# Attention and two expert stages on one core: new numbers in a planner that sets each engine's order, with other costs for short products and for routing

## The chip, the core and the metric

The kernel runs on one NeuronCore of a Trainium2 chip. Five engines work side by side, each through its own queue in program order: PE (TensorE, matrix products and transposes into PSUM), DVE (VectorE), ACT (ScalarE), POOL (GpSimd, which also issues the indirect transfers), and SP (SyncE, which issues the other transfers). An engine whose next instruction waits for a semaphore does nothing else, whatever stands behind it. The metric is the device time of one execution in microseconds (us); less is better.

## The reference

Three parts in a row. The third sends each of the 3072 tokens to one of 8 experts with 384 places each, in the order of the gate's values.

```python
# attention: 4 x 8 heads, 768 positions, 64 wide
k_sum = k.reshape(B, H, nb, 32, D).max(axis=3)
v_sum = v.reshape(B, H, nb, 32, D).mean(axis=3)
scores_s = scale * np.einsum('bhsd,bhnd->bhsn', q, k_sum) + np.log(32)
scores_l = np.where(np.abs(pos[:, None] - pos[None, :]) < 16, scale * np.matmul(q, k.transpose(0, 1, 3, 2)), -1e9)
a = softmax(np.concatenate([scores_l, scores_s], axis=-1))
x = np.matmul(a, np.concatenate([v, v_sum], axis=2))     # then to 3072 x 512
...
x = (((x @ w1) * (x @ w2)) @ w3) @ w_out                 # 512 -> 1024 -> 1024 -> 512
...
# experts: logits = x @ w_gate; largest values first, a token once, 384 tokens to an expert
for e in range(8):
    out[mask_e] = np.maximum(x[mask_e] @ w1[e], 0.0) @ w2[e]
```

## The kernel before, in words

The big products are exact to float32 by splitting each operand into a high and a low float32r part (`x_h`, `x_l` for the activations, `w12_h`, `w12_l` for w1 and w2, `split_e` for expert weights) and adding three products, h·h, h·l and l·h. A long product is 128x512 (or 128x384, 128x256); the short ones are attention's, the transposes and routing's.

**Stages.** Attention runs in 16 head pairs of 3 steps, 48 steps `n`. Per pair: `transposes` of K and Q on PE into banks 0 and 1, then `evac_kmax` and `evac_kedge` on DVE and `evac_k`, `evac_q` on ACT, which empty those banks. Per two steps `s_mm` (scores). Per step: `s_min` (DVE), four `s_exp1` (ACT), `s_inv` (DVE), `s_norm` (POOL), `p_tr` (transpose on PE into bank 4), `p_evac` (ACT, out of bank 4). Per two steps `pv_mm`, then two `xt` copies. Once all steps that touch a chunk of 512 tokens are done for a head pair kt (0 to 3), `x_h` (ACT) and `x_l` (DVE) make its two parts, and `ab_mm(c, ft, m, kt)` multiplies it by w1 (m=0) and w2 (m=1): six chunks c, eight column tiles ft, three long products a call. `ab_a` and `ab_b` empty their banks. In the same stretch the 64-bit w1 and w2 words are narrowed (`narrow_y` on ACT, `narrow` on DVE).

Then w3·w_out is multiplied out (`wmm`), the logits are made, and routing runs: seven searches by bisection, each of three or four rounds of `compare` (DVE), `count` (PE), `full` (DVE), `count_full` (PE), `narrower` (DVE), with `bound` behind the first round, and `which_full`, `spread_full` (PE), `choose` (DVE) at the end of a search. In the gaps PE takes `row_mm`, the products that give the experts' input rows: 480 of 512 columns (t up to 19) and then 192 of 256 columns. Each finished tile is put (`row_put`, ACT) and stored to DRAM (`row_store`, SP); `gather` (POOL) fetches the rows of an expert in two halves of three transfers, once `places_end` (DVE) has the indices. Behind routing come `turn` (transposes of gathered rows), `up_mm`, `down_mm`, `scatter` for eight experts.

**What sets the order.** All operations are put in a list with a time of their own, `t`, an engine, a duration and the names that they read and write. `schedule` plays this list through: each engine that is free takes the ready operation with the smallest `t`, and is then busy for the duration. The order in which they were taken is emitted, engine by engine; nothing is reordered on the chip. `t` comes from the step, from `CFG` and from `OFF`, one number per function. `CFG` also says which engine takes a copy (`xdve`, `pdve`, `kedge`, `xl`, `wl12`).

Of the kernel before, what the change touches and what calls it, by code (L numbers as in the profile page):

```python
# [46 lines left out]
SHARED = ("narrow", "vb_sum", "x_l", "s_sub", "s_half", "s_norm", "k_spread", "wconv_l", "w12_l", "abh_l", "split_e", "wph_put")  # L47


def schedule(ops, free):  # L50
# [39 lines left out]
    now, done, port = 0.0, [], 0.0  # L90
# [25 lines left out]
def fused_kernel(tc, q, k, v, moe_w1, moe_w2, moe_w3, moe_w_out, w_gate, ew1, ew2, out):  # L116
    nc = tc.nc
    with ExitStack() as ctx:
# [167 lines left out]
        def evac_q(j):  # L286
            nc.scalar.activation(QT[j % 2], turned_qk("q", j)[:, 0:768], AF.Copy, scale=-0.125)
# [262 lines left out]
        for j in range(-1, NJ):  # L550
# [8 lines left out]
            if J < NJ:  # L559
# [14 lines left out]
            for n in range(m, m + 3):  # L574
                P, SB, VB_ = ("P", n % NP), [s_bank(0), s_bank(1)], pv_bank(n)
                if n % 2 == 0:
                    kq = [(x, i % 2) for i in sorted({n // 3, (n + 1) // 3}) for x in ("Kw", "Ke", "Kg", "Ks", "Q")]
                    op(n, PE, 1.02, kq, SB, s_mm, n // 2)
# [3 lines left out]
                if not C["pacc"] or n % C["pacc"]:  # L582
# [11 lines left out]
                dve = C["pdve"] and n % C["pdve"] == 0  # L594
# [774 lines left out]
```

## Time and profile before

| what | value |
|---|---|
| time, median of 3 runs | 943.7 us (941.36 to 944.99) |
| the profiled execution | 939.69 us, its span 937.9 us |
| PE busy | 879.5 us, 94% of the span |
| DVE, ACT, POOL busy | 482.0, 408.7, 262.1 us |
| TensorE's granted clock, mean | 0.99 |

The span runs from the first to the last instruction. A granted clock of 1.00 is 2.4 GHz and 0.50 is 1.2 GHz; a value between is a mean over a stretch with both. PE is called busy while a product or transpose is in it, so a share of 94% says where PE waits, not that its work could not be quicker.

### The profile page before, as it was taken

Reading aid. Unit: us, or ns where it says so; the run is one execution under the profiler, and the core shown is the slowest. Engines: PE = TensorE matmul, PEld = TensorE weight load, DVE = VectorE, ACT = ScalarE, POOL = GpSimd, SP = SyncE. Lnnn points to the kernel's source line nnn. Section 1 sums busy time; section 2 is a strip of 40 time slices with the busy share of each in tenths; the row PEclk is TensorE's granted clock in tenths of the full one; section 3 lists DMA queues with packets and bytes.
Section 4 is the critical chain, followed back from the end, with each engine's and each line's share of the span. In section 5 each row is a group of like instructions: output and inputs, shape, how many; then the busy total and the mean of one; then the engine's idle time right before and its main releaser. Section 6 shows DMA issues by size and latency. Waiting matters only on the chain.

```text
span 937.9 us, 16023 instructions
## 1 busy us (share of the span) xinstructions
PE 879.5 (94%) x5899; PEld 731.2 (78%) x5899; DVE 482.0 (51%) x1351; ACT 408.7 (44%) x987; POOL 262.1 (28%) x280
## 2 busy tenths in 40 slices
PE   2687999999999999999999999999999999999994
PEld 2465887888888887777776667689898998899893
DVE  4887997846556641111316666663465355445110
ACT  1787888985443251111224142322465345445220
POOL 4535344432011000000027384535513313301001
PEclk9989999999999999999999999999999999999997
DMA  9999988733343200000003134113656446454001
GB/s 231 224 213 206 226 191 158 153 82 110 116 120 122 74 1 1 1 0 1 1 1 113 61 120 135 35 45 96 199 209 216 135 157 207 142 169 147 23 13 36
DMA packets 143335, 105.22 MB, mean 112 GB/s; under 512 B 103312, under 2 KB 117648, under 8 KB 143248
## 3 DMA queue, kind: packets, MB, share of 16 engines
q1 hardware_dynamic: 139024, 91.53, 36.4%
q0 software_dynamic: 4224, 12.59, 3.8%
q8 instruction: 48, 0.79, 0.4%
q14 instruction: 39, 0.32, 0.1%
HBM read 89.15 MB, written 12.58 MB: 108 GB/s over the span
## 4 chain that ended last, share of the span: by engine, by line
PE 84%; DVE 7%; DMA 3%; ACT 2%; SPq 1%; issue 1%; POOL 0%; POOLq 0%; ACTq 0%; DVEq 0%
PE PS L499 28%; PE PS L1233 14%; PE PS L1247 13%; PE PS L1127 11%; PE PS L448 5%; PE PS L373 2%; PE PS L358 2%; PE PS L318 2%; PE PS L265 2%; PE PS L633 1%; DMA w_dt.float<-in_k_dram 1%; PE PS L1217 1%; DVE w_dt.float L853 1%; PE PS L435 1%; PE PS L465 1%
## 5 line engine op out<-in xcount | busy, mean ns | idle before, releaser
L499 PE MATMUL PS<-w_dt.float32r,w_dt.float32r 128*128 128x512 f32 x1152 | 283.4, 397 | 0.6 <-ACT w_dt.float L269 0.4
L499 PEld LDWEIGHTS PS<-w_dt.float32r,w_dt.float32r 128*128 128x128 f32 x1152 | 210.7, 188 | 50.4 <-issue 7.1
L1127 PE MATMUL PS<-w_dt.float32r,w_dt.float32r 128*128 128x512 f32 (+1 forms) x672 | 143.9, 367 | 0.0
L1233 PE MATMUL PS<-w_dt.float32r,w_dt.float32r 128*128 128x384 f32 x768 | 135.5, 335 | 0.9 <-ACT w_dt.float32r L1222 0.5
L1233 PEld LDWEIGHTS PS<-w_dt.float32r,w_dt.float32r 128*128 128x128 f32 x768 | 133.4, 188 | 2.4 <-ACT w_dt.float32r L1222 1.0
L1247 PE MATMUL PS<-w_dt.float32r,w_dt.float32r 128*128 128x512 f32 x576 | 135.0, 392 | 0.0
L1104 POOL TENSOR_TENSOR w_dt.float32r<-w_dt.float,w_dt.float32r 128x512 fp32r<-128x512 f32 x48 | 61.4, 1301 | 240.9 <-issue 185.6
L1247 PEld LDWEIGHTS PS<-w_dt.float32r,w_dt.float32r 128*128 128x128 f32 x576 | 107.0, 188 | 21.7
L1127 PEld LDWEIGHTS PS<-w_dt.float32r,w_dt.float32r 128*128 128x128 f32 x672 | 109.6, 190 | 15.8 <-issue 0.8
L1184 DVE TENSOR_TENSOR w_dt.float32r<-w_dt.float,w_dt.float32r 128x512 fp32r<-128x512 f32 x112 | 72.3, 687 | 61.5 <-ACT w_dt.float32r L1182 60.5
L506 DVE TENSOR_TENSOR w_dt.float<-w_dt.float,PS 128x512 f32<-128x512 f32 x48 | 32.9, 686 | 121.3 <-PE PS L499 117.1
L1182 ACT ACTIVATE w_dt.float32r<-w_dt.float 128x512 fp32r<-128x512 f32 x128 | 73.6, 625 | 15.2 <-DMA w_dt.float<-in_moe_w_dram 11.3
L502 ACT ACTIVATE w_dt.float<-PS 128x512 f32<-128x512 f32 x48 | 28.6, 597 | 114.3 <-PE PS L499 114.2
L335 ACT ACTIVATE w_dt.float<-w_dt.float,w_dt.float 128x120 f32<-128x120 f32 x192 | 73.7, 388 | 4.3 <-DVE w_dt.float L324 4.3
L1241 DVE SCALAR_TENSOR_TENSOR w_dt.float32r<-PS,w_dt.float32r 128x384 fp32r<-128x384 f32 x64 | 35.5, 556 | 74.2 <-ACT w_dt.float32r L1239 74.2
L1202 POOL DMA_INDIRECT w_dt.float<-moe_rows,w_dt.float x48 | 47.1, 981 | 84.6 <-PE PS L1217 65.4
L354 POOL TENSOR_TENSOR w_dt.float<-w_dt.float,w_dt.float 128x480 f32<-128x480 f32 x48 | 50.6, 1058 | 61.1 <-DVE w_dt.float L351 47.4
L1254 POOL DMA_INDIRECT out_dram<-w_dt.float,w_dt.float x24 | 25.2, 1049 | 139.1 <-ACT w_dt.float L1251 126.3
L1100 ACT ACTIVATE w_dt.float32r<-w_dt.float 128x1024 fp32r<-128x1024 f32 x24 | 25.3, 1058 | 83.6 <-PE PS L1127 60.4
L1239 ACT ACTIVATE w_dt.float32r<-PS 128x384 fp32r<-128x384 f32 x64 | 31.3, 489 | 65.9 <-PE PS L1233 65.8
L265 PE MATMUL PS<-w_dt.float,w_dt.float 128*128 128x128 f32 x192 | 30.9, 304 | 23.4 <-DMA w_dt.float<-in_k_dram 14.8
L448 PE MATMUL PS<-w_dt.float32r,w_dt.float32r 128*128 128x512 f32 x192 | 48.1, 395 | 0.0
(154 smaller groups left out, 1035.3 us busy)
## 6 DMA issues: line engine op xcount, KB each, us to landing
w_dt.float<-in_moe_w_dram SPq DMA_DIRECT2D x128, 256.0 KB
w_dt.float<-in_moe_w_dram SPq DMA_DIRECT2D x32, 512.0 KB
w_dt.float<-in_v_dram SPq DMA_DIRECT2D x32, 240.0 KB
w_dt.float<-in_v_dram SPq DMA_DIRECT2D x32, 192.0 KB
w_dt.float<-in_k_dram SPq DMA_DIRECT2D x32, 192.0 KB
w_dt.float<-in_q_dram SPq DMA_DIRECT2D x32, 192.0 KB
moe_rows<-w_dt.float SPq DMA_DIRECT2D x48, 128.0 KB
w_dt.float<-in_moe_w_out_dram SPq DMA_DIRECT2D x8, 512.0 KB
```

Source lines behind the costliest of these rows:

```text
L265: nc.tensor.transpose(trp[:, g * 128:(g + 1) * 128], stage[kind][j % 2][:, g], ident)
L335: nc.scalar.activation(PR[n % NP][:, u], PR[n % NP][:, u], AF.Exp, bias=st[n % NP][:, 0, u:u + 1], scale=-1.0, accum_out=st[n % NP][:, 1, ...
L354: nc.gpsimd.tensor_mul(PR[n % NP], PR[n % NP], st[n % NP][:, 2].unsqueeze(2).to_broadcast([128, 4, 120]))
L448: nc.tensor.matmul(PS[:, (5, 4)[it % 2]], w[:, i // 2, i % 2], WO[i][hl], start=i == 0 and s == 0, stop=i == 3 and s == 2)
L499: nc.tensor.matmul(PS[:, ab_bank(c, ft, m)], a[:, kt], x[:, kt], start=kt == 0 and s == 0, stop=kt == 3 and s == 2)
L1104: nc.gpsimd.tensor_sub(l[:, i:i + 4], ab_of(t)[:, i:i + 4], h[:, i:i + 4].bitcast(F32))
L1127: nc.tensor.matmul(PS[:, row_bank(t, half), row_cols(half)], a[:, kt], b[:, row_cols(half)], start=kt == 0 and s == 0, stop=kt == 7 and s ...
L1182: nc.scalar.activation(h, f, AF.Copy)
L1184: (nc.gpsimd if e == 0 else nc.vector).tensor_sub(l, f, h.bitcast(F32))
L1202: nc.gpsimd.indirect_dma_start(out=xg[e % 2][:, i, half * 256:half * 256 + 256], out_offset=None, in_=xs[half], in_offset=bass.IndirectOff ...
L1233: nc.tensor.matmul(PS[:, up_bank(e, ft), 0:384], a, b[:, kt], start=kt == 0 and s == 0, stop=kt == 3 and s == 2, skip_group_check=e == 0)
L1247: nc.tensor.matmul(PS[:, 6 + i % 2], a[:, ft, ts], b, start=ft == 0 and s == 0, stop=ft == 7 and s == 2)
```

## The change

It does four things. (1) `CFG` and `OFF` get new numbers for nearly every function, so the `t` of nearly every operation changes: `pv_mm` goes from -3.737 to -18.884, `s_norm` from -0.819 to -17.403, `ab_mm` from -3.135 to -5.075, `x0` (the first chunk's `x_h` and `x_l`) from 13.789 to 15.11. (2) The durations that the planner reckons with are changed for attention's products and transposes and for routing's DVE operations, and each long product that follows a short one on PE is charged 0.1. (3) One engine for a whole kind of copy becomes a list with an entry a step: `pa`, `pe`, `qe`, `ke` (all entries 0: the engine that it was) and `xe` (a 1 at every third step, as `xdve=3` had it). (4) Two engine lists differ: in `wl12` the last entry goes from 1 to 0 (the low part of w2's last tile from POOL to DVE), in `xl` the fourth from 0 to 1 (`x_l` of chunk 3, four subtractions, from DVE to POOL).

```diff
+LONG = ("ab_mm", "wmm", "row_mm", "up_mm", "down_mm")
...
                 end = now + ops[i][2]
+                if e == 1:
+                    name = getattr(ops[i][5], "__name__", "") in LONG
+                    end += 0.1 * (name and not long)
+                    long = name
...
-                op(m + C["k"], PE, 0.655, [("st", "k", J % 2, 0), ("st", "k", J % 2, 1), "ident"], [0, 1], transposes, "k", J)
+                op(m + C["k"], PE, 0.75, [("st", "k", J % 2, 0), ("st", "k", J % 2, 1), "ident"], [0, 1], transposes, "k", J)
...
-                    op(n, PE, 1.02, kq, SB, s_mm, n // 2)
+                    op(n, PE, 1.06, kq, SB, s_mm, n // 2)
...
-                op(n, PE, 1.10, vr + [("PT", (n - 1) % 3), ("PT", n % 3)], [VB_], pv_mm, n // 2)
+                op(n, PE, 1.14, vr + [("PT", (n - 1) % 3), ("PT", n % 3)], [VB_], pv_mm, n // 2)
...
-                    dve = C["xdve"] and i % C["xdve"] == 0
+                    dve = C["xe"][i]
...
-                op(RT, DVE, 0.99, [7, "m", "kw", "lo", "bounds"], ["cmp"], compare, i, it)
+                op(RT, DVE, 1.02, [7, "m", "kw", "lo", "bounds"], ["cmp"], compare, i, it)
...
-                    op(RT + 1, DVE, 0.45, [7, "kw"], [6, "bounds"], bound, i)
+                    op(RT + 1, DVE, 1.0, [7, "kw"], [6, "bounds"], bound, i)
...
-            op(RT, DVE, 1.5, ["lo"], [7, "Lm", "m", "Ah"], choose, False)
+            op(RT, DVE, 2.0, ["lo"], [7, "Lm", "m", "Ah"], choose, False)
```

**What moves: ACT, steps 2 and 3 of attention.** Before: L335 is `s_exp1` (w_51776 is step 5's tile, w_11776 step 6's, w_15872 step 7's), L274 `evac_k` of pair 3, L269 into w_24192 and w_53056 `p_evac` of steps 2 and 3, L287 `evac_q` of pair 3, L406 `narrow_y`, L486 `w12_h`.

```order
L486 ACTIVATE w_35968_dt.float32r<-w_36480_dt.float_113 128x512
L274 ACTIVATE w_15392_dt.float_68<-PS 128x10x96
L269 ACTIVATE w_24192_dt.float_93<-PS 120x512
L406 ACTIVATE w_30336_dt.float_379<-w_30336_dt.float_379 128x512
L406 ACTIVATE w_6784_dt.float_241<-w_6784_dt.float_241 128x512
L335 ACTIVATE w_11776_dt.float_89,w_1664_dt.float_59<-w_11776_dt.float_89,w_1664_dt.float_59 128x120
L287 ACTIVATE w_52544_dt.float_70<-PS 128x768
L335 ACTIVATE w_11776_dt.float_89,w_1664_dt.float_59<-w_11776_dt.float_89,w_1664_dt.float_59 128x120
L335 ACTIVATE w_15872_dt.float_90,w_1664_dt.float_59<-w_15872_dt.float_90,w_1664_dt.float_59 128x120
L335 ACTIVATE w_11776_dt.float_89,w_1664_dt.float_59<-w_11776_dt.float_89,w_1664_dt.float_59 128x120
L335 ACTIVATE w_15872_dt.float_90,w_1664_dt.float_59<-w_15872_dt.float_90,w_1664_dt.float_59 128x120
L269 ACTIVATE w_53056_dt.float_91<-PS 120x512
```

The same place now (lines have moved by 8 to 11):

```order
L497 ACTIVATE w_35968_dt.float32r<-w_36480_dt.float_113 128x512
L346 ACTIVATE w_51776_dt.float_88,w_1664_dt.float_59<-w_51776_dt.float_88,w_1664_dt.float_59 128x120
L277 ACTIVATE w_24192_dt.float_93<-PS 120x512
L282 ACTIVATE w_15392_dt.float_68<-PS 128x10x96
L417 ACTIVATE w_30336_dt.float_378<-w_30336_dt.float_378 128x512
L277 ACTIVATE w_53056_dt.float_91<-PS 120x512
L346 ACTIVATE w_11776_dt.float_89,w_1664_dt.float_59<-w_11776_dt.float_89,w_1664_dt.float_59 128x120
L417 ACTIVATE w_6784_dt.float_241<-w_6784_dt.float_241 128x512
```

`p_evac` of step 2 stood behind `evac_k` of pair 3 and now stands ahead of it, and `p_evac` of step 3 is no longer behind one `narrow_y`, `evac_q` of pair 3 and six `s_exp1` of steps 6 and 7 (one of them stands ahead of the piece that is shown).

**What moves: PE, the first long products.** Before, behind `s_mm` of steps 10 and 11: L499 is `ab_mm` (w_34944 and w_35456 the high and low part of w1's first tile, w_35968 and w_36480 those of w2's), L358 `p_tr` of step 7, L373 `pv_mm` of steps 6 and 7.

```order
L318 MATMUL PS<-w_15392_dt.float_68,w_52544_dt.float_70 64x120 x16
L499 MATMUL PS<-w_3712_dt.float32r,w_34944_dt.float32r 128x512
L499 MATMUL PS<-w_5760_dt.float32r,w_34944_dt.float32r 128x512
L499 MATMUL PS<-w_3712_dt.float32r,w_35456_dt.float32r 128x512
L358 MATMUL PS<-w_1664_dt.float_59,w_15872_dt.float_90 120x128 x4
L499 MATMUL PS<-w_3712_dt.float32r,w_35968_dt.float32r 128x512
L499 MATMUL PS<-w_5760_dt.float32r,w_35968_dt.float32r 128x512
L499 MATMUL PS<-w_3712_dt.float32r,w_36480_dt.float32r 128x512
L373 MATMUL PS<-w_53056_dt.float_91,w_31872_dt.float_85 64x64 x8
L373 MATMUL PS<-w_20096_dt.float_92,w_31872_dt.float_85 64x64 x8
```

Now, from `pv_mm` of steps 6 and 7 on, with `p_tr` of step 8 and `s_mm` of steps 12 and 13 behind it:

```order
L384 MATMUL PS<-w_53056_dt.float_91,w_31872_dt.float_85 64x64 x8
L384 MATMUL PS<-w_20096_dt.float_92,w_31872_dt.float_85 64x64 x8
L369 MATMUL PS<-w_1664_dt.float_59,w_51296_dt.float_87 120x128 x4
L329 MATMUL PS<-w_11296_dt.float_67,w_34176_dt.float_69 64x120 x16
L510 MATMUL PS<-w_3712_dt.float32r,w_34944_dt.float32r 128x512
L510 MATMUL PS<-w_5760_dt.float32r,w_34944_dt.float32r 128x512
L510 MATMUL PS<-w_3712_dt.float32r,w_35456_dt.float32r 128x512
L510 MATMUL PS<-w_3712_dt.float32r,w_35968_dt.float32r 128x512
L510 MATMUL PS<-w_5760_dt.float32r,w_35968_dt.float32r 128x512
L510 MATMUL PS<-w_3712_dt.float32r,w_36480_dt.float32r 128x512
L369 MATMUL PS<-w_1664_dt.float_59,w_51776_dt.float_88 120x128 x4
```

The first long products come one `s_mm` and one `pv_mm` later. When `pv_mm` of steps 10 and 11 is reached, 18 long products stood ahead of it and 6 stand there now, and `s_mm` of steps 14 and 15, which stood ahead of it, follows it. At `pv_mm` of steps 14 and 15 it is 54 against 60, at the last one 309 against 282. Long products come in 48 runs in attention in both, and in 36 from there to the first `row_mm` in both.

**What moves: PE, a `choose` gap in routing.** Before: L889 is `spread_full`, L859 the `count` behind the next `compare`, L1127 `row_mm`; 16 of these stand between.

```order
L889 MATMUL PS<-w_53200_dt.float_128 128x8
L1127 MATMUL PS<-w_35968_dt.float32r,w_43648_dt.float32r 128x512
L1127 MATMUL PS<-w_36480_dt.float32r,w_43648_dt.float32r 128x512
...
L1127 MATMUL PS<-w_40064_dt.float32r,w_44672_dt.float32r 128x512
L1127 MATMUL PS<-w_41088_dt.float32r,w_43648_dt.float32r 128x512
L859 LDWEIGHTS w_53200_dt.float_128
```

Now, with 18 between:

```order
L900 MATMUL PS<-w_53200_dt.float_128 128x8
L1138 MATMUL PS<-w_34944_dt.float32r,w_44672_dt.float32r 128x512
L1138 MATMUL PS<-w_35968_dt.float32r,w_43648_dt.float32r 128x512
...
L1138 MATMUL PS<-w_41088_dt.float32r,w_43648_dt.float32r 128x512
L1138 MATMUL PS<-w_41600_dt.float32r,w_43648_dt.float32r 128x512
L870 LDWEIGHTS w_53200_dt.float_128
```

All six `choose` gaps go from 16 to 18 `row_mm`, all seven gaps behind `bound` from 11 to 13, and the gaps ahead of the first `count` from 10, 8 and 12 to 9, 8 and 11. Some gaps of the last search take more as well. Behind the last `places_turn` 63 of the 256-column products are left where there were 106, 43 fewer. DVE's order in routing is the same word for word, and so is POOL's order of the gathers: three for expert 0, three for expert 1, three for expert 2, all of the first half, and then expert 0's second half. With the experts, each of the six later changes of expert has its transposes in three pieces of 6, 3 and 3 where it had two of 6. SP's order is the same for its first 34 rows.

## Rows read from the trace of the kernel before

**Rows 1.** Busy time by stretch: length, each engine's busy us (instructions), granted clock.

```profile
0.00:19.00 19.00, 3.68 (x16) 3.29 (x17) 8.10 (x28) 1.28 (x1) 8.58 (x26) 1.00 1.01 213
48.00:52.00 4.00, 3.68 (x42) 3.11 (x42) 3.48 (x19) 2.95 (x9) 0.56 (x1) 0.59 1.24 222
58.00:61.30 3.30, 3.28 (x38) 2.88 (x38) 2.83 (x10) 2.38 (x7) 1.28 (x1) 0.52 1.03 212
61.30:77.00 15.70, 13.24 (x182) 10.21 (x179) 14.17 (x58) 14.21 (x52) 8.06 (x10) 0.99 0.92 208
77.00:95.00 18.00, 14.21 (x184) 11.12 (x185) 13.18 (x39) 13.43 (x38) 9.65 (x12) 1.00 0.99 197
95.00:240.00 145.00, 143.64 (x1599) 116.73 (x1598) 107.87 (x442) 115.37 (x380) 56.06 (x63) 1.00 0.68 152
498.00:635.00 137.00, 129.72 (x777) 99.27 (x775) 91.56 (x294) 41.70 (x59) 75.60 (x60) 1.00 0.24 79
```

**Rows 2.** Timeline of PE, attention: start, length, idle before in brackets.

```profile
48.31 1.08 PE L358 MATMUL PS<-w_dt.float,w_dt.float 128*120 128x128 f32 x4 [2.63 <-ACT w_dt.float L269]
49.18 1.49 PE L265 MATMUL PS<-w_dt.float,w_dt.float 128*128 128x128 f32 x6
...
52.95 1.30 PE L373 MATMUL PS<-w_dt.float,w_dt.float 120*64 120x64 f32 x32
...
61.91 0.82 PE L265 MATMUL PS<-w_dt.float,w_dt.float 128*128 128x128 f32 x6
...
78.34 1.05 PE L318 MATMUL PS<-w_dt.float,w_dt.float 64*64 64x120 f32 x32
...
93.57 0.87 PE L265 MATMUL PS<-w_dt.float,w_dt.float 128*128 128x128 f32 x6 [2.16 <-DVE w_dt.float L271]
```

**Rows 3.** The chain that ended last, 45 to 48 us: start, length, what.

```profile
45.71 0.97 DVE w_dt.float L280
...
46.70 0.97 ACT w_dt.float L274
```

**Rows 4.** Timeline of ACT, 48 to 54 us.

```profile
48.05 1.23 ACT L406 ACTIVATE w_dt.float<-w_dt.float 128x512 f32<-128x512 f32 x2
49.16 0.40 ACT L335 ACTIVATE w_dt.float<-w_dt.float,w_dt.float 128x120 f32<-128x120 f32 x1
...
50.70 0.81 ACT L287 ACTIVATE w_dt.float<-PS 128x768 f32<-128x768 f32 x1 [1.05 <-PE PS L265]
...
52.92 0.58 ACT L269 ACTIVATE w_dt.float<-PS 120x512 f32<-120x512 f32 x1
```

**Rows 5.** Who PE waited for, routing: us in total, times, longest.

```profile
PE PS L859 <- DVE w_dt.float L853: 5.4, 8, 1.3
```

**Rows 6.** Timeline of PE: a long run, and routing.

```profile
459.57 20.68 PE L499 MATMUL PS<-w_dt.float32r,w_dt.float32r 128*128 128x512 f32 x90
...
525.44 0.32 PE L859 MATMUL PS<-w_dt.float 128*128 128x32 bf16 x6 [1.17 <-DVE w_dt.float L853]
...
530.32 0.31 PE L859 MATMUL PS<-w_dt.float 128*128 128x32 bf16 x6 [0.24 <-DVE w_dt.float L853]
...
634.96 12.97 PE L1127 MATMUL PS<-w_dt.float32r,w_dt.float32r 128*128 128x256 f32 x106
647.76 0.82 PE L1217 MATMUL PS<-w_dt.float,w_dt.float 128*128 128x128 f32 x6
```

**Rows 7.** Timelines of DVE and POOL: the last index, first and third gather.

```profile
635.37 0.18 DVE L941 SCALAR_TENSOR_TENSOR w_dt.float<-PS,w_dt.float 128x24 int32<-128x24 f32 x1
...
639.67 1.16 POOL L1202 DMA_INDIRECT w_dt.float<-moe_rows,w_dt.float  x1 [8.59 <-PE PS L1127]
...
642.39 0.95 POOL L1202 DMA_INDIRECT w_dt.float<-moe_rows,w_dt.float  x1 [0.30 <-issue]
```

**Rows 8.** Timeline of PE, expert 0's change to 1.

```profile
670.63 0.49 PE L1217 MATMUL PS<-w_dt.float,w_dt.float 128*128 128x128 f32 x3
670.88 0.94 PE L1247 MATMUL PS<-w_dt.float32r,w_dt.float32r 128*128 128x512 f32 x3
```

More of the change, by code (lines that the diff above doesn't have):

```diff
@@ new lines @@
+OFF = dict(up_mm=-32.743, scatter=3.361, turn=3.442, abh_h=14.838, up_put=-18.011, split_e=-25.911, load_e=-37.338, down_put=1.355, row_put=51.973, abh_l=5.475, down_mm=-21.553, row_mm=-23.679, row_store=-22.747, wph_put=6.513, gather=14.179, turn_put=-14.47, no_rows=19.111, k_spread=20.863, p_evac=6.15, w12_h=3.199, wconv_l=-9.694, g_tr=34.329, wtr=-10.647, s_min=-0.217, s_mm=1.56, s_exp1=-0.174, x_h=2.227, wtr_evac=4.983, logits=-6.577, pv_mm=-18.884, evac_k=4.305, g_put=9.635, g_mm=-13.019, s_norm=-17.403, v_spread=7.787, vb_mean=28.542, evac_q=12.658, wload=28.461, x_l=-2.049, wp_add=-0.062, logit_copy=32.145, xt=-5.548, w12_l=-0.002, load_qk=3.45, s_inv=-0.845, evac_kedge=-32.689, load_v=-13.884, load_w12=-1.79, g_evac=15.894, evac_kmax=9.037, p_tr=-6.196, narrow_y=6.585, logit_sum=-10.479, ab_mm=-5.075, narrow=-0.227, wconv_h=14.634, ab_b=-5.388, load_vb=-4.303, wmm=-18.171, vb_sum=39.734, wp_evac=-41.709, transposes=-16.506, ab_a=-7.715, logit_tr=20.195)
@@ L89, in schedule @@
             heapq.heappush(ready[ops[i][1]], (ops[i][0], i))
-    now, done, port = 0.0, [], 0.0
+    now, done, port, long = 0.0, [], 0.0, False
     while len(done) < len(ops):
@@ L286, in evac_q @@
         def evac_q(j):
-            nc.scalar.activation(QT[j % 2], turned_qk("q", j)[:, 0:768], AF.Copy, scale=-0.125)
+            if CFG["qe"][j]:
+                nc.vector.tensor_scalar(QT[j % 2], turned_qk("q", j)[:, 0:768], -0.125, None, op0=OP.mult)
+            else:
+                nc.scalar.activation(QT[j % 2], turned_qk("q", j)[:, 0:768], AF.Copy, scale=-0.125)
         def v_spread(j):
@@ L563, in fused_kernel @@
                 qb = [0, 1] if J else [4, 5]
-                op(m + C["k"], PE, 0.655, [("st", "k", J % 2, 0), ("st", "k", J % 2, 1), "ident"], [0, 1], transposes, "k", J)
+                op(m + C["k"], PE, 0.75, [("st", "k", J % 2, 0), ("st", "k", J % 2, 1), "ident"], [0, 1], transposes, "k", J)
                 op(m + C["k"], DVE, 0.93, [0, 1], [("Kg", J % 2)], evac_kmax, J)
                 op(m + C["k"], ACT, 0.87, [0, 1], [("Kw", J % 2)], evac_k, J)
-                op(m + C["k"], ACT if C["kedge"] else DVE, 0.31 if C["kedge"] else 0.27, [0, 1], [("Ke", J % 2)], evac_kedge, J)
+                op(m + C["k"], (DVE, ACT)[C["ke"][J]], (0.27, 0.31)[C["ke"][J]], [0, 1], [("Ke", J % 2)], evac_kedge, J)
                 op(m + C["k"], (DVE, POOL, ACT)[C["kpool"]], (0.37, 0.55, 0.33)[C["kpool"]], [("Kg", J % 2)], [("Ks", J % 2)], k_spread, J)
-                op(m + C["q"], PE, 0.655, [("st", "q", J % 2, 0), ("st", "q", J % 2, 1), "ident"], qb, transposes, "q", J)
-                op(m + C["q"], ACT, 0.78, qb, [("Q", J % 2)], evac_q, J)
+                op(m + C["q"], PE, 0.75, [("st", "q", J % 2, 0), ("st", "q", J % 2, 1), "ident"], qb, transposes, "q", J)
+                op(m + C["q"], DVE if C["qe"][J] else ACT, 0.90 if C["qe"][J] else 0.78, qb, [("Q", J % 2)], evac_q, J)
             if j < 0:
@@ L581, in fused_kernel @@
                 pu = [P + (u,) for u in range(4)]
-                if not C["pacc"] or n % C["pacc"]:
+                if not C["pa"][n]:
                     for u in range(4):
@@ L593, in fused_kernel @@
                 op(n, PE, 0.46, pu, [4], p_tr, n)
-                dve = C["pdve"] and n % C["pdve"] == 0
+                dve = C["pe"][n]
                 op(n, DVE if dve else ACT, 0.65 if dve else 0.54, [4], [("PT", n % 3)], p_evac, n, 0 if dve else 2)
@@ L1059, in fused_kernel @@
                 op(RT, PE, 0.12, ["some", "first"], [6], count_full)
-                op(RT, DVE, 0.17, [7, "kw", "bounds"], [6, "lo"], narrower, i, it)
+                op(RT, DVE, 0.22, [7, "kw", "bounds"], [6, "lo"], narrower, i, it)
                 if it == 0:
-                    op(RT + 1, DVE, 0.45, [7, "kw"], [6, "bounds"], bound, i)
-            op(RT, DVE, 0.2, [], [6, "chosen"], which_full)
+                    op(RT + 1, DVE, 1.0, [7, "kw"], [6, "bounds"], bound, i)
+            op(RT, DVE, 0.34, [], [6, "chosen"], which_full)
             op(RT, PE, 0.12, ["cond", "chosen"], [7], spread_full)
-            op(RT, DVE, 1.5, ["lo"], [7, "Lm", "m", "Ah"], choose, False)
+            op(RT, DVE, 2.0, ["lo"], [7, "Lm", "m", "Ah"], choose, False)
             op(RT + 1, DVE, 0.07, [], [7, "capv"], close)
```

5 lines of the change are left out of this document (2 added, 3 removed).

## The prediction

> **What bounds the kernel now.** I read the busy time by stretch first. PE works without a pause for most of the span; it waits at the start for the first keys (15.3 of the first 19.0 us), in attention's first part (2.5 us in 61.3 to 77, 3.8 us in 77 to 95), for 1.4 us between 95 and 240, and in routing (7.3 us in 498 to 635) [rows 1]. Everywhere else the time is PE's own work, which the change leaves as it is, product by product. So a new order can give or take only in three ways: PE waits less or more, products run at another clock, or the changes between long and short products cost more or less. The first 34 rows of SP are the same, so the start stays. The end behind the last product isn't touched.
>
> The timeline of PE shows what the waits are. At 48.31 `p_tr` of step 3 has waited 2.63 us for ACT, and what follows runs slowly: six transposes take 1.49 us, and 0.82 at 61.91 [rows 2]. The granted clock says why: 0.59 in 48 to 52 and 0.52 in 58 to 61.3, that is near 1.2 GHz, where the neighbours show 2.4 [rows 1]. At that place the chain goes through `evac_kmax` of pair 3 on DVE, 0.97 us, and `evac_k` on ACT, 0.97 us [rows 3], and only then comes `p_evac` of step 2, which frees bank 4 for `p_tr`.
>
> **The engine lists.** `pa`, `pe`, `qe`, `ke` are all zeros and `xe` repeats what stood there, so no step changes its engine. The two other edits move one subtraction to DVE and four to POOL in stretches where PE has no wait that leads to them. I price this part at nothing. Were it uncovered, one subtraction more on DVE would be under 1 us.
>
> **A, attention's first part.** `p_evac` of step 2 no longer stands behind `evac_k`, so `p_tr` of step 3 is rid of the two pieces of 0.97 us [rows 3]. `p_evac` of step 3, at 52.92, loses what stood ahead of it: six `s_exp1` of some 0.39 us (one takes 0.40; its accumulator read lies largely under the next), one `narrow_y` of 0.6 (two take 1.23) and `evac_q` of 0.81, 3.7 us together [rows 4]. `pv_mm` of steps 2 and 3, at 52.95 [rows 2], could then be up to 3.7 us earlier; transposes and their copies still stand ahead of it, so I take 3.0 (bounds 0 and 3.7). What is late next are the steps whose exponentials were pushed back, 6 and 7, and the first chunk's `x_h` and `x_l`.
>
> The price: when `pv_mm` of steps 10 and 11 is reached, 12 long products and one `s_mm` are still to do that were done before. A long product takes 20.68/90 = 0.23 us [rows 6], so 2.8 us, and `s_mm` 1.0 [rows 2]. Up to there PE has waited 3.0 less by the clock on the wall but has done 3.8 less: +0.8 us. From there on more long products stand ready, and the order has 60 of them instead of 54 by `pv_mm` of steps 14 and 15. The waits of 77 to 95 (3.8 us, 2.16 of them before the transposes at 93.57 [rows 2]) and of 95 to 240 (1.4) have something to be filled with. PE takes its instructions in order, though, and DVE and ACT are busy 13.2 and 13.4 of these 18 us [rows 1]. I take half, -1.9 and -0.7 (bounds all and nothing).
>
> The clock: at full level the work of 48 to 52 would take 3.68 x 0.59 = 2.2 us and that of 58 to 61.3 3.28 x 0.52 = 1.7, so the two slow stretches hold 1.5 + 1.6 = 3.1 us. They follow PE's waits, and the order shortens the first of these. But PE isn't alone on the path there, so I take half of one stretch, -0.7 (bounds -3.1 and +1.6, one stretch more). Sum of A: 0.8 - 1.9 - 0.7 - 0.7 = -2.5; bounds -8.2 (0.1 - 3.8 - 1.4 - 3.1) and +5.4 (3.8 + 1.6).
>
> **B, the gaps of routing.** `count` waited 8 times, 5.4 us in total [rows 5]. Four of these waits lie behind `choose` (1.17 at 525.44 is one; 4.2 together), three behind `bound` (0.24 at 530.32 is one; 0.6 together), one at the start [rows 5, 6]. Each of these gaps gets two more `row_mm`, 0.46 us. That takes 0.46 from each of the four and the whole 0.6, so -2.4. In gaps where PE didn't wait, DVE gets its counts later by as much, but PE has done work that it must do anyway: no cost, since nothing waits for DVE there but PE itself. The start has two products fewer between `logit_tr` and the first `count`: +0.4. Sum -2.0. The bounds are 0 and -2.4.
>
> **C, behind routing.** The work that B takes forward was cover here. Behind the last `places_turn` 106 half products take 12.97 us, 0.122 each; 63 take 7.7, up to 642.7 on the old time line [rows 6]. The gathers were held until 639.67 by the last stores of the first half's rows [rows 7]; these now lie far ahead, and the indices are written at 635.55. With the pause of 0.30 that POOL shows, the first gather starts at 635.9, the third 2.7 later at 638.6. From the third gather's start at 642.39 to the first `turn` at 647.76 it took 5.4 us [rows 6, 7]. So `turn` can start at 644.0, and PE waits 1.3 us. Queued behind it stand expert 0's `up_mm`; and the gathers of expert 2, which stand ahead of expert 0's second half, wait for these transposes too, at the same distance as before. Bounds: 0 (the gathers land sooner) and +5.2 (the first starts no earlier, relative to the end of the half products). The page DMA: Bandwidth & Descriptors of the Trainium skill (section on the SWDGE path) gives 2.0 us and bytes over 436 GB/s for such a transfer, 2.3 us for 128 KB; by it PE would not wait here and the sum would be 1.3 us less. The 5.4 us of the row decides.
>
> **D, the experts.** Six times a run of transposes is cut once more. Three transposes take 0.25 us at 670.63, and the three long ones behind them start at 670.88 [rows 8]: next to no loss. I put 0.05 for each, +0.3 (bounds 0 and 0.6, the planner's own 0.1).
>
> **Sum.** -2.5 - 2.0 + 1.3 + 0.3 = -2.9 us, on the profiled 939.69: 936.8. The runs' median lies 4.0 us above that execution, and the difference carries over: 943.7 - 2.9 = 940.8 us. About 0.5%, 4.7 us, is what a measurement of this kernel can tell from no change.
>
> **Rivals.** *The front clears (faster).* Attention is ahead by the full 3.7, PE finds long products wherever it waited between 77 and 240, and both slow stretches go: A is -8.2, the sum -8.6, 935 us. For it: each wait there names ACT or DVE work that the order moves. Against: ACT is busy 14.2 of 15.7 us in 61.3 to 77 [rows 1], and the same work must pass. Chance 0.34.
>
> *The clock (slower).* PE has only short products and waits until `s_mm` of steps 12 and 13. If the low level holds through 61.3 to 77, where it was 0.99, the short products there, 13.24 less 18 long ones at 0.23, so 9.1 us, take 9.1 more; 2.5 of waits absorb a part, and A's gain of 2.5 is gone: -2.9 + 6.6 + 2.5 = +6.2, 950 us. It decides once PE stands idle again for as long as before 48.31 in that stretch. For it: the first long products come later. Against: the order feeds PE sooner around 50. The page TensorE: Matmul & The Clock Gate of the Trainium skill (Why this matters for your kernels) says that idle gaps between bursts bring the clock back to half; by that rule the change, which takes long products out of the sparse part, is a risk, and the trace agrees with 0.59 behind 2.63 us of idling. Chance 0.08.
>
> *Nothing comes of the front.* The planner's steps are ahead on paper, `x_l` of the first chunk is late on DVE, and PE's queue stands at the second `ab_mm` with short products behind it: A is +3 instead of -2.5, the sum +2.6, 946 us. Chance 0.14.
>
> The forecast's own case has 0.44, and lies in 938 to 943.
>
> **Range and chances.** From 935 (the front clears) to 947 (nothing comes of it) leaves out the clock, the far end of the faster case and a late gather at once with a bad front: 2 in 10. Faster by over 0.5% (under 939.0): 0.34 and a tenth of the forecast's case, together 0.38. Slower (over 948.4): the clock's 0.08 and a third of the third rival, 0.13. Within: 0.49.
>
> **What would show it.** A: `p_tr` of step 3 waits under 1 us; PE's idle time from 61.3 to 95 falls below 6.2 us; the granted clock in 45 to 62 is above the 0.5s. B: `count`'s waits sum to some 3 us. C: the first `turn` waits 1 to 2 us for a gather, and a longer wait would prove the gather chain mispriced. D: `down_mm` and `turn` show the same time an expert within 0.1 us. I'm wrong if the difference comes from 240 to 492, where I see none, or if PE's busy time there differs by over 1 us.

## The result, and the profile after

The changed kernel takes 951.25 us (median of 19 runs, 945.92 to 960.41) against 944.33 for the kernel before on the same chips; the ratio is 1.0078, 95% interval 1.006 to 1.0097. It is 7 us slower where 3 us faster was forecast. The profiled execution took 945.92 us (span 944.0), 6.2 more than that of before (939.69). PE's last product ends at 931.57 instead of 925.08, and 4.9 of these 6.5 us are longer waits of PE.

Busy time by stretch of the changed kernel, the same columns as [rows 1]:

```profile
0.00:19.00 19.00, 3.89 (x18) 3.67 (x19) 7.80 (x28) 1.28 (x1) 8.68 (x26) 0.71 1.01 220
48.00:52.00 4.00, 3.71 (x77) 2.90 (x75) 3.55 (x19) 4.00 (x16) 1.86 (x3) 1.00 1.24 236
58.00:61.30 3.30, 1.74 (x35) 1.30 (x36) 3.27 (x9) 3.30 (x11) 3.13 (x3) 1.00 1.16 241
61.30:77.00 15.70, 11.98 (x156) 9.55 (x158) 12.60 (x53) 10.91 (x32) 7.24 (x13) 0.89 1.15 206
77.00:95.00 18.00, 16.82 (x180) 13.31 (x180) 15.73 (x57) 15.45 (x51) 8.24 (x8) 1.00 1.10 237
95.00:240.00 145.00, 142.34 (x1591) 114.24 (x1590) 105.93 (x427) 113.88 (x375) 52.36 (x61) 1.00 0.64 147
240.00:498.00 258.00, 255.69 (x1247) 202.10 (x1247) 84.84 (x133) 68.01 (x122) 15.96 (x12) 1.00 0.12 39
498.00:635.00 137.00, 129.61 (x742) 99.74 (x741) 88.30 (x285) 43.26 (x62) 76.86 (x62) 1.00 0.25 83
```

The row for 240 to 498 of the kernel before:

```profile
240.00:498.00 258.00, 258.00 (x1264) 204.54 (x1264) 90.31 (x144) 70.63 (x125) 12.44 (x12) 1.00 0.13 42
```

In 240 to 498, where PE never waited before, it waits 2.3 us. The two slow stretches of [rows 1] are gone (1.00 and 1.00), but 0 to 19 shows 0.71 and 61.3 to 77 shows 0.89: the granted clock was 0.50 from 8.1 to 35.3 and from 66.1 to 69.4. Whom PE waited for from 240 to 640 (us, times, longest):

```profile
PE PS L870 <- DVE w_dt.float L864: 6.2, 6, 1.8
PE PS L476 <- ACT w_dt.float L472: 2.3, 2, 1.6
PE PS L848 <- DVE w_dt.float L845: 1.2, 1, 1.2
```

The first row answers to [rows 5]: `count` waits 6.2 us instead of 5.4. The second is new. L476 is `g_mm`, the product behind the transposes of the folded gate weights, and L472 `g_evac`, the evacuation on ACT between them. The timeline there:

```profile
329.36 2.97 POOL L405 TENSOR_TENSOR w_dt.float32r<-w_dt.float,w_dt.float32r 128x512 fp32r<-128x512 f32 x2 [41.84 <-ACT w_dt.float32r L401]
...
332.36 1.16 ACT L401 ACTIVATE w_dt.float32r<-w_dt.float 128x512 fp32r<-128x512 f32 x2 [1.82 <-POOL w_dt.float32r L405]
...
335.51 0.59 ACT L472 ACTIVATE w_dt.float<-PS 128x512 f32<-128x512 f32 x1
...
336.15 1.06 PE L476 MATMUL PS<-w_dt.float,w_dt.float 128*128 128x8 f32 x8 [1.65 <-ACT w_dt.float L472]
...
339.74 1.06 PE L476 MATMUL PS<-w_dt.float,w_dt.float 128*128 128x8 f32 x8 [0.66 <-ACT w_dt.float L472]
```

L405 on POOL is `x_l` of chunk 3, one of the two edits of the engine lists. `x_h` (L401) waits for it, `g_evac` stands behind `x_h` in ACT's queue, and PE waits for `g_evac`.

PE's waits by stage in the two profiles (added up from PE's timeline, the kernel before first): up to the last `pv_mm` 37.44 and 36.50; from there to the last `ab_mm` 0 and 2.31; to the last `places_turn` 7.28 and 7.93; to the first `down_mm` 0.87 and 3.72; behind it 0 and 0. From the first `down_mm` to PE's end it takes 256.61 and 256.75 us.

### The profile page after: what moved, and what is told of

It reads as the page before. It is cut to its first block, busy times and chain, and to the rows that moved or that the text cites. A ratio compares the mean times of both kernels' runs of the same rounds, so it can differ in the third digit from the quotient of the medians.

```text
span 944.0 us, 16025 instructions
## 1 busy us (share of the span) xinstructions
PE 881.1 (93%) x5899; PEld 730.4 (77%) x5899; DVE 480.6 (51%) x1348; ACT 406.7 (43%) x987; POOL 264.9 (28%) x283
## 4 chain that ended last, share of the span: by engine, by line
PE 79%; DVE 8%; ACT 4%; DMA 3%; issue 2%; SPq 1%; POOL 1%; another core or an unknown queue 0%; POOLq 0%; ACTq 0%; DVEq 0%
PE PS L510 25%; PE PS L1244 14%; PE PS L1258 13%; PE PS L1138 11%; PE PS L459 5%; ACT w_dt.float L346 2%; PE PS L369 2%; PE PS L384 2%; PE PS L273 2%; PE PS L329 1%; DMA w_dt.float<-in_k_dram 1%; PE PS L644 1%; DMA w_dt.float<-in_moe_w_dram 1%; PE PS L1228 1%; DVE w_dt.float L262 1%
## 5 line engine op out<-in xcount | busy, mean ns | idle before, releaser
L1115 POOL TENSOR_TENSOR w_dt.float32r<-w_dt.float,w_dt.float32r 128x512 fp32r<-128x512 f32 x48 | 61.6, 1307 | 197.9 <-PE PS L510 145.8
L1195 DVE TENSOR_TENSOR w_dt.float32r<-w_dt.float,w_dt.float32r 128x512 fp32r<-128x512 f32 x112 | 72.0, 688 | 57.1 <-ACT w_dt.float32r L1193 38.4
```

Of the source, the lines that this page charges most:

```text
L1115: nc.gpsimd.tensor_sub(l[:, i:i + 4], ab_of(t)[:, i:i + 4], h[:, i:i + 4].bitcast(F32))
L1195: (nc.gpsimd if e == 0 else nc.vector).tensor_sub(l, f, h.bitcast(F32))
```

## The experiments

Each is compared with runs of the kernel before on the same chip (942 us in the median each time), so a ratio of 1.0000 means no change. `nolow` alone is a single run and is read by its trace.

### One half each

The numbers in `CFG` and `OFF` fall apart into those of attention and the stretch to the last `ab_mm`, and those of routing and the experts, so each half can be had alone.

```diff
 # h_front: open/after with the later numbers and routing's durations of before
-... row_mm=-23.679, turn=3.442, gather=14.179, ... LONG = (all five)
+... row_mm=-49.599, turn=-6.762, gather=15.039, ... LONG = ("ab_mm", "wmm")
 # h_back: the reverse, with LONG = ("row_mm", "up_mm", "down_mm")
```

> Attention and the stretch up to the last ab_mm in the changed order, routing and experts in the old one (the first 2,718 instructions of PE's queue are the changed kernel's, the rest the old kernel's). Theory 1, each half pays its own part: the two profiles put the last ab_mm 3.05 us later (492.36 and 495.41), so 3 us slower than before. Theory 2, as predicted: the front gains 2.5 us and the loss comes from behind, so 2.5 us faster than before.

> The reverse: attention in the old order, routing and experts in the changed one. Theory 1: 3.4 us slower than before (the end of PE moved by 6.49 us, 3.05 of them in the front). Theory 2, as predicted: 0.4 us faster (-2.0 in the gaps, +1.3 behind routing, +0.3 in the experts).

`h_front`: ratio 1.0060 (1.0040 to 1.0079), +4.4 us in the medians. `h_back`: 1.0038 (1.0015 to 1.0060), +3.6. Both halves are slower, and within the intervals they make up the whole; theory 2 falls in both places.

### The engine edit

```diff
-xl=(0, 0, 0, 1, 0, 0)
+xl=(0, 0, 0, 0, 0, 0)
```

> The changed kernel with x_l of chunk 3 back on DVE; the orders of PE and ACT stay instruction for instruction. Theory 1: the slow subtractions on POOL hold x_h on ACT, behind it the evacuation before logits, and so PE (1.65 and 0.66 us): 2.3 us faster than the changed kernel, and the two waits are gone. Theory 2, as priced: no difference, PE waits there for ACT anyway.

> The kernel before with x_l of chunk 3 on POOL and nothing else; the orders of PE and ACT stay. Theory 1: POOL's 1.29 us against 0.69 hold x_h on ACT and the evacuations behind it, PE waits 1 to 2.3 us more near 335: 1 to 2.3 us slower than before. Theory 2, as priced in the prediction: no difference.

> The half with attention in the changed order, with x_l of chunk 3 back on DVE; the orders of PE and ACT stay. Theory 1, the engine edit is half of that half's loss (4.4 us): 2 us slower than before, with one wait of 1.2 us left near 340. Theory 2, the loss is all attention's own order: still 4 to 5 us slower than before.

`xl0` is at 1.0066 of before (1.0037 to 1.0095), about 1 us under the changed kernel; the waits for `g_evac` fall from 2.31 to 1.17, not to 0. `before_xl`, which is the kernel before with this edit alone, is at 1.0025 (1.0002 to 1.0048), with a wait of 0.75 us in that place. `front_xl0` gained nothing on `h_front` (1.0061, 1.0041 to 1.0082), though its wait also fell, from 2.32 to 1.18. So the edit costs PE 0.75 to 1.15 us of waiting with all orders of PE and ACT unchanged. In time the three pairs put it at 2.3 us (`before_xl`), 1.1 (`xl0`) and nothing (`front_xl0`), each uncertain by 2 us or more, so the waiting is shown and the time is not. The other list edit, the last entry of `wl12`, was not tried by itself.

### What holds DVE in routing

In the gap behind `choose` PE has 18 `row_mm` now and was to wait 0.46 us less than before. In the third search it waits longer (1.80, before 1.34):

```profile
556.15 4.33 PE L1138 MATMUL PS<-w_dt.float32r,w_dt.float32r 128*128 128x512 f32 x18
562.27 0.32 PE L870 MATMUL PS<-w_dt.float 128*128 128x32 bf16 x6 [1.80 <-DVE w_dt.float L864]
```

The cause stands in DVE's rows for routing, 503 to 632 us (line, operation, count, busy us, mean ns):

```profile
L860 DVE TENSOR_TENSOR w_dt.float<-w_dt.float 128x1 f32<-128x1 f32 x7 | 6.3, 901 | 0.1
L823 DVE TENSOR_TENSOR w_dt.float<-w_dt.float 128x192 bf16<-128x192 f32 x6 | 5.2, 860 | 0.2
L893 DVE SCALAR_TENSOR_TENSOR w_dt.float<-w_dt.float 128x7 f32<-128x7 f32 (+6 forms) x7 | 4.7, 675 | 0.2
L820 DVE SCALAR_TENSOR_TENSOR w_dt.float<-w_dt.float 128x192 f32<-128x192 f32 x6 | 4.1, 676 | 0.2
```

A subtraction of one element a partition (L860, in `search_start`) takes 901 ns on average; single ones take 0.16 or 0.98. The same four lines in the kernel before, in the same order:

```profile
L849 DVE TENSOR_TENSOR w_dt.float<-w_dt.float 128x1 f32<-128x1 f32 x7 | 3.0, 433 | 0.1
L812 DVE TENSOR_TENSOR w_dt.float<-w_dt.float 128x192 bf16<-128x192 f32 x7 | 4.9, 694 | 0.2
L882 DVE SCALAR_TENSOR_TENSOR w_dt.float<-w_dt.float 128x7 f32<-128x7 f32 (+6 forms) x7 | 5.3, 750 | 0.2
L809 DVE SCALAR_TENSOR_TENSOR w_dt.float<-w_dt.float 128x192 f32<-128x192 f32 x7 | 5.4, 766 | 0.2
```

All four read two tensors in SBUF. Of these operations in the changed kernel's routing 18 are long and 11 short. Beside each long one a subtraction of POOL runs (`abh_l`, or the low part of `split_e`, both of some 1.3 us); of the short ones 8 have none beside them, and 3 had begun before POOL's.

```diff
         def abh_l(t, i):
+            if 2 <= t < 22:
+                return
```

> The changed kernel without POOL's subtractions for tiles 2 to 21 of the rows (their low parts stay those of an older tile). Theory 1: DVE's slow operations in the gaps of choose and bound are held by POOL's, so they all take their short time (0.36, 0.16, 0.22) and count's waits, 6.2 us, fall under 1 us. Theory 2: these operations are slow by themselves or by what PE reads; the waits stay at 5 to 6 us.

`count`'s waits fall to 0.84 us and the span to 939.5 (944.0), in one run. POOL's subtractions are what holds DVE. In `h_back` the hold was longest; a timeline of three engines (L1115 is `abh_l`, L1195 `split_e`):

```profile
553.29 2.58 POOL L1115 TENSOR_TENSOR w_dt.float32r<-w_dt.float,w_dt.float32r 128x512 fp32r<-128x512 f32 x2
554.60 3.98 DVE L820 SCALAR_TENSOR_TENSOR w_dt.float<-w_dt.float 128x192 f32<-128x192 f32 x1
555.78 2.59 POOL L1195 TENSOR_TENSOR w_dt.float32r<-w_dt.float,w_dt.float32r 128x512 fp32r<-128x512 f32 x2
...
562.55 0.34 PE L870 MATMUL PS<-w_dt.float 128*128 128x32 bf16 x6 [4.25 <-DVE w_dt.float L864]
```

DVE's operation of 0.36 us took 3.98, to just behind the end (558.37) of POOL's subtractions that are shown, and PE waited 4.25. To test that it is the two SBUF inputs, each of the four operations got one operand in PSUM:

```diff
-scalar_tensor_tensor(t8, Lm, lo, PS[:, 7, 0:8]...)
-scalar_tensor_tensor(Lm, t8, -1.0e38, Lm, ...)
-tensor_reduce(m, a, ...); tensor_tensor(Ah, a, m..., op=OP.is_equal)
+scalar_tensor_tensor(tp, Lm, lo, PS[:, 7, 0:8]...)
+scalar_tensor_tensor(Lm, tp, -1.0e38, Lm, ...)
+tensor_reduce(mp, a, ...); tensor_tensor(Ah, a, mp..., op=OP.is_equal); tensor_copy(m, mp)
-tensor_sub(w, lo if i else hi, bounds[:, i:i + 1])
+tensor_scalar(wp, lo if i else hi, bounds[:, i:i + 1], None, op0=OP.subtract)
 # tp, mp, wp (and up, the last input of bound) are columns of PS[:, 7]
```

> The kernel before, with choose's scratch, its maxima, search_start's difference and the last input of bound in PSUM (bank 7), so that these operations of DVE no longer read two tensors in SBUF; one small copy more in each choose. Theory 1, POOL's subtractions hold exactly the operations with two SBUF inputs: they take 0.36, 0.36, 0.16 and 0.22 us again, count's waits fall from 5.4 us to about 1, and the kernel is 4 us faster than before. Theory 2, any operation of DVE that writes or reads SBUF is held: no change of the waits.

> The changed kernel with the same four operations on PSUM. Theory 1: count's waits fall from 6.2 us to under 1, so 5 us faster than the changed kernel, and level with the kernel before with the same edit or within the front's loss of it (+4). Theory 2: no change.

`ps_before`: ratio 0.9923 (0.9898 to 0.9948), 934.54 us, 7 us faster than the kernel before. It beats both kernels. `ps_after`: 0.9999 (0.9974 to 1.0024), so 7 us faster than the changed kernel, and 7 us slower than `ps_before`, where theory 1 had 4 at the most. The same four operations in `ps_before`, and the only wait of PE left from 498 to 640:

```profile
L814 DVE TENSOR_TENSOR w_dt.float<-w_dt.float,PS 128x192 bf16<-128x192 f32 x8 | 2.8, 354 | 0.3
L811 DVE SCALAR_TENSOR_TENSOR w_dt.float<-PS,w_dt.float 128x192 f32<-128x192 f32 x7 | 2.5, 358 | 0.2
L885 DVE SCALAR_TENSOR_TENSOR w_dt.float<-PS,w_dt.float 128x7 f32<-128x7 f32 (+6 forms) x7 | 1.6, 222 | 0.2
L852 DVE TENSOR_SCALAR PS<-w_dt.float 128x1 f32<-128x1 f32 x7 | 1.6, 222 | 0.3
```

```profile
PE PS L940 <- DVE w_dt.float L926: 0.4, 1, 0.4
```

`count` waits nowhere any more, and PE's waits from the last `ab_mm` to the last `places_turn` are 0.42 us instead of 7.28: 6.9 us, about the measured 7. Theory 1 had 4 us, from `count` alone, whose 5.4 us are gone. Another 1.4 were waits ahead of two other products (0.93 before `range_spread`, 0.51 before `places_before`). The edit moves a few products as well (10 `row_mm` instead of 8 ahead of `range_spread`), so this part isn't the hold's alone. The page SBUF — State Buffer of the Trainium skill (Who interferes with whom) says that an operation of DVE with two SBUF inputs contends with one of GpSimd that reads SBUF and one with at most one such input, outside the two-port modes, does not, and the runs agree: 0.36 against up to 3.98 us. That the second one waits until the first finishes, as the summary of that page of the Trainium skill (rules for kernel authors) has it, is too short here: 3.98 us is three of POOL's subtractions.

### Routing and experts without that hold

```diff
 # ps_back: h_back with the four operations on PSUM
```

> Attention in the old order, routing and experts in the changed one, with the four operations of routing on PSUM: beside the kernel before with the same edit (7 us faster than before) it differs by the changed routing and experts alone, and nothing in routing waits any more. Theory 1, what is left of the back's loss is the shorter cover behind routing: transposes of expert 0's second half wait 1.5 us for their gather, with a slow stretch of the clock behind it in a part of the runs (1.7): 5 us faster than before. Theory 2, the back's loss was POOL's hold alone: 7 us faster than before, as without the changed order.

Ratio 0.9988 (0.9968 to 1.0007), where `ps_before` has 0.9923: routing and experts in the changed order cost about 6 us here (3 to 9 with both intervals, and the two ran on different chips), with next to no wait in routing in either (0.53 and 0.42 us). From the last `places_turn` to the first `down_mm` PE waits 6.12 us in this profile instead of 0.88:

```profile
PE PS L1247 <- ACT w_dt.float32r L1236: 4.1, 1, 4.1
PE PS L1247 <- issue: 1.6, 2, 1.4
PE PS L1231 <- DMA w_dt.float<-moe_rows,w_dt.float: 0.5, 1, 0.5
```

So the back's loss without the hold lies behind routing, as theory 1 had it, but only the last row is a wait for a gather. The first is an engine that goes on late, told at the end, and its cause is open. That the shorter cover is the reason for all 6 us is not shown. In `ps_after` the wait for the gather is plain: the transposes of expert 0's second half wait for the gather of the same half.

```profile
656.42 0.33 PE L1231 MATMUL PS<-w_dt.float,w_dt.float 128*128 128x128 f32 x1 [0.63 <-DMA w_dt.float<-moe_rows,w_dt.float]
657.59 0.66 PE L1231 MATMUL PS<-w_dt.float,w_dt.float 128*128 128x128 f32 x4 [0.84 <-DMA w_dt.float<-moe_rows,w_dt.float]
```

Such a wait (0.5 to 1.5 us) stands in five of the six profiles with the changed back, and in none of the eight with the old one. The sixth, the changed kernel's own, has another one there, shown at the end. Against the 0.87 us of the old order, PE waits 0.9, 0.9, 1.0 and 1.5 us more behind routing in `h_back`, `nolow`, `xl0` and `ps_after`, and 2.9 and 5.3 more in the changed kernel and `ps_back`, where an engine goes on late.

### Attention alone

```diff
 # fw2: h_front with xl[3]=0, and s0, so, g0, xs and the offsets of the w3 x w_out stage as before
-op(t, ACT, 0.575, raws, [("xh", c, kt)] + al, x_h, c, kt)
+op(t, ACT, 0.575, raws + [("wg", it) for it in range(8) if c > 2], ...)   # fw3a alone
```

> Attention's changed numbers alone: those of the product of w3 and w_out, of the gate's weights behind it, and of x_h's start are the old ones, x_l of chunk 3 is on DVE; routing and experts as before. Theory 1, attention's new order neither gains nor loses and the front's loss (4.4 us) is the wait of the gate's products near 340 with what follows: level with before (0 to 1 us). Theory 2, attention's order itself costs the time by the clock in its first 100 us: 4 us slower than before.

> The kernel with attention's changed numbers alone, and x_h of chunks 3 to 5 put behind the whole chain of the gate's weights on ACT, so that the evacuations that PE waits for near 340 stand behind no x_h; PE's order up to there stays. Theory 1, what was left of the front's loss (3.9 us) is that wait of 1.2 us with the fall of the clock behind it: the wait is gone, and the kernel is within 2 us of before. Theory 2, attention's order costs the time in its own stretch: the wait is gone, and it is still 3 to 4 us slower than before.

`fw2`: 1.0042 (1.0019 to 1.0065), and 1.18 us of waiting for `g_evac` remain. `fw3a`: 1.0028 (1.0010 to 1.0046), +2.6 us (between the theories); 0.79 us of waiting remain, where it was to be gone. These don't settle it by themselves. PE's waits up to the last `pv_mm` do say something: 35.61 to 39.35 us in the six profiles with the old attention (mean 37.6), 36.50 to 39.08 in the eight with the new one (mean 37.4). The new order gains no waiting there. Up to the last `ab_mm` the means of all profiles but `waits8` are 495.2 us with the old attention (five) and 497.8 with the new one (eight). Of the 2.6 us between them 1.2 are waits and 1.4 PE's busy time. Single profiles lie 8 us apart, so this shows where to look and no more.

### What a wait costs

```diff
+def ping(): nc.tensor.transpose(PS[:, 7, 0:128], lt[:, 0:128], ident)
+def pong(): four activation(lt, PS[:, 7], AF.Copy)
+# in ab_mm's loop, c in (3, 4), ft in (2, 3, 6, 7): ping, pong, ping
```

> The kernel before with eight waits added to PE, in the stretch of long products between 345 and 490: a transpose, four copies on ACT (2.3 us) and a second transpose, with three long products between (0.7). Theory 1, a wait there costs more than its length since the clock falls behind it at times: the eight waits are some 2 us each, 16 together, 2 us for the transposes, and each fall that follows costs 1.7: 20 to 30 us slower than before. Theory 2, a wait costs its length alone: 16 to 18 us, and the granted clock stays at 1.00 there.

967.87 us, ratio 1.0265 (1.0231 to 1.0298), +25.6. Waits from 345 to 520 us, the timeline of the first, and the stretches behind five of them (columns as in [rows 1]):

```profile
PE PS L646 <- ACT w_dt.float L650: 15.8, 8, 2.2
```

```profile
373.96 0.33 PE L646 MATMUL PS<-w_dt.float 128*128 128x128 f32 x1 [1.94 <-ACT w_dt.float L650]
374.05 6.62 PE L499 MATMUL PS<-w_dt.float32r,w_dt.float32r 128*128 128x512 f32 x21
```

```profile
345.00:374.40 29.40, 27.46 (x171) 18.91 (x164) 4.14 (x6) 8.12 (x17) 0.00 (x0) 1.00 0.00 1
374.60:377.80 3.20, 3.20 (x9) 2.49 (x8) 0.00 (x0) 0.00 (x0) 0.00 (x0) 0.50 0.00 0
384.90:388.10 3.20, 3.20 (x9) 2.43 (x9) 0.00 (x0) 0.60 (x1) 0.00 (x0) 0.50 0.00 0
405.40:408.60 3.20, 3.20 (x9) 2.43 (x9) 0.00 (x0) 0.00 (x0) 0.00 (x0) 0.50 0.03 5
415.60:418.80 3.20, 3.20 (x9) 2.52 (x8) 0.00 (x0) 0.60 (x1) 0.00 (x0) 0.50 0.00 0
473.60:476.80 3.20, 3.20 (x9) 2.49 (x8) 0.00 (x0) 0.80 (x2) 0.00 (x0) 0.50 0.02 5
```

Behind five of the eight waits (seven of 1.94 us, one of 2.21) the granted clock is 0.50 for 3.4 us, which costs half of that. 15.8 of waits, five times 1.7, and 16 transposes of 0.09 (373.96 to 374.05) are 25.7; the medians differ by 25.6. That the two agree so closely is luck, for the profiled run is the slowest of the six (971.95). A wait of 2 us among long products costs some 3 on average here; shorter waits were not tried this way.

## Why the prediction was wrong, point by point

**The engine lists, priced at nothing.** Wrong for `xl`: "in stretches where PE has no wait that leads to them" was read from the old trace, where `x_l` took 0.69 us on DVE. At 1.29 on POOL it is on the path through ACT. The step failed because the wait that an edit makes can't stand in the trace of before; ACT's queue behind `x_h` does, and was not looked at. In its place stand 0.75 to 1.15 us of waiting through this edit and 2.3 us at `g_mm` in all.

**A, attention (-2.5).** The place was read rightly and two of A's three signs came true. `p_tr` of step 3 waits 1.21 us instead of 2.63 (under 1 was forecast), `pv_mm` of steps 2 and 3 starts at 48.18 instead of 52.95, 61.3 to 95 holds 4.9 us of waits instead of 6.2, and the granted clock from 45 to 62 is 1.00. The steps that failed are the "-0.7" for 95 to 240, where the waits rose from 1.4 to 2.7, and 52 to 77, which has no term: they rose from 2.6 to 4.0 up to 61.3, and from 2.5 to 3.7 from there. In 77 to 95 they fell by 2.6, more than the 1.9 of the sum. So the work that was pushed back became late in its turn, as the third rival had it. The last `pv_mm` ends 5.9 us earlier, but 27 long products, 6.2 us at 0.23, are then still to do: nothing is left of the lead. The opening sentence "Everywhere else the time is PE's own work" was wrong too: from 19 to 61.3 us PE waited 14.5 us. It waits 13.8 there now, so this miss cost the forecast little.

The front's +4.4 us is explained in part. 2.3 us stand at `g_mm`, where the prediction saw no difference and called one a sign of being wrong: about half through `xl`, the rest through attention's order (`fw2`, which has the later numbers of before, keeps 1.18). Four of the eight profiles with the new front have a stretch of 3.4 or 6.8 us at 0.50 within 3 us behind that wait, none of the five with the old one; the changed kernel's own has none, though it has both waits. 2.3 and about 1 us for these are 3.3 of 4.4. The rest stays open, and `fw2` and `fw3a`, slower by 4.0 and 2.6 us with 1.2 and 0.8 us of waiting there, leave room for a loss in attention itself.

**B, routing's gaps (-2.0).** Measured +0.8 in `count`'s waits. The waits behind `bound` (0.24, 0.24, 0.15) are gone, as foreseen. The step that failed is "That takes 0.46 from each of the four": it holds where DVE's chain kept its length (1.17 to 0.68), but the shift by two `row_mm` a gap also moves `abh_l`, which follows `row_mm` by way of ACT, against DVE's chain, and other operations of DVE met it. `search_start`'s subtraction was long in 6 of 7 searches where it had been in 2, and the four lines' busy time went from 18.6 to at least 20.3 us, two of them with one operation fewer in the count. The chain's length was taken as fixed. That operations with two SBUF inputs wait for POOL at all stood in no term.

**C, behind routing (+1.3).** The step that failed is "From the third gather's start at 642.39 to the first `turn` at 647.76 it took 5.4 us", taken for what a gather needs. Up to 647.9 PE was busy with the 106 half products, so these 5.4 us are PE's own work; the third gather landed 2.9 us after its start. All gathers of the kernel before:

```profile
DMA to landing us min/median/max: 2.6/3.8/8.2
```

With 2.9 the third one, started at 638.6, would have landed ahead of 642.7, without a wait; and the first `turn` waits for no gather in any profile. Expert 0's second half does, 0.5 to 1.5 us in five of six, and of it the prediction said only "at the same distance as before". That this is the size of the +1.3 is luck. The 2.9 and 5.3 us in the two profiles with a late engine were in no term, and the cause is open. "These now lie far ahead", of the last stores of the first half, came true: the last is issued at 638.53 and landed at 640.21, while the indices are written at 643.90. The first gather starts at 644.87, 0.97 us behind them and not 0.3.

**D, the experts (+0.3).** Right: 256.61 and 256.75 us from the first `down_mm` to PE's end, 0.14 for six more cuts.

**The rivals.** The clock's rival came out nearest in time (950), by luck: there was no long loss in 61 to 77, where one stretch of 3.4 us is at 0.50. Falls of 3.4 us behind new waits among long products, which no term of the sum held, took a part instead. Of the mechanisms, "nothing comes of the front" was nearest for attention, and got 0.14. The page TensorE: Matmul & The Clock Gate (Why this matters for your kernels) of the Trainium skill warns of idle gaps; I weighed it for attention alone, and the falls at `g_mm` and in `waits8` came where PE is dense. The range (935 to 947) ended at the third rival because every later term was taken at its length in waits.

## What to carry to other kernels

A wait of PE among long products can cost more than its length: eight waits of 2 us cost half as much again here, which a forecast should hold as a term. When a plan moves work on PE, look at what follows it on POOL, and at which operations of DVE read two SBUF tensors; one operand in PSUM freed four small operations and gave 7 us, where tuned orders gave none. A row that tells when an engine went on doesn't tell when its input was there: before taking a distance for a transfer's time, see whether the engine was busy with other work. A planner that reckons only with durations lets the shortest cover shrink until a transfer shows: keep slack behind the last index for the gathers of both halves.

## What the runs showed that was not expected

- Engines go on late in two profiles. In the changed kernel the transposes behind the last `row_mm` start at 650.94 in the trace, but ACT and POOL, which wait for these two, go on only at 653.62 and 653.99:

```profile
650.94 0.82 PE L1228 MATMUL PS<-w_dt.float,w_dt.float 128*128 128x128 f32 x6
...
653.62 0.38 ACT L1145 ACTIVATE w_dt.float<-PS 128x256 f32<-128x256 f32 x1 [2.90 <-remote]
...
653.99 0.95 POOL L1213 DMA_INDIRECT w_dt.float<-moe_rows,w_dt.float  x1 [1.37 <-remote]
...
654.44 0.44 PE L1244 MATMUL PS<-w_dt.float32r,w_dt.float32r 128*128 128x384 f32 x1 [2.68 <-ACT w_dt.float32r L1233]
```

  `ps_back` has the same at 653.57 (ACT goes on at 657.74, PE waits 4.05). Both lie among the gathers. Whether PE's signals come late or the trace has PE's times too early, it can't tell; the cause stays open.
- A stretch of 27.3 us (once 23.9) at 0.50 from 8 or 9 us on stands in 8 of the 14 profiles, six of them with the new front. Over all runs a mean clock under 0.98, which mostly goes with it, is no more frequent with the new front (36 of 86 runs) than with the old one (71 of 141), so nothing shows that the change costs time by it. PE mostly waits there, and among the kernel before's 24 runs of one chip those with a mean clock under 0.98 took 942.0 us on average, the others 940.9.
- The runs of the changed kernel scatter more (standard deviation 4.2 us against 1.3 for before on the same chips, without one run of 1264.51), as falls behind waits would make them; that link wasn't tested by itself.
